# First transform of the fifth to eighth batch: three f16 products in place of one f32 product

## The chip, the cores and the metric

The kernel runs on one core of a Trainium2 chip. The metric is the device time of one execution in microseconds (us). The engines are TensorE (PE; its weight loads are listed as PEld), VectorE (DVE), ScalarE (ACT), GpSimd (POOL) and SyncE (SP, which here issues transfers).

## The reference

A two-dimensional Fourier transform is taken of each of 8 batches, its real part is kept, and the 19,968 rows go through a mixture of 8 experts, one expert for each row.

```python
X = np.fft.fft(x, axis=1)                 # x: (8, 2496, 256)
X = np.fft.fft(X, axis=2)
x = X.real.reshape(19968, 256)
logits = x @ w_gate;  e_idx = argmax(logits)
eom = sigmoid(x @ w_output_gate)
for e in range(8):
    h = np.maximum(x[mask] @ w1[e], 0.0)  # (rows, 1024)
    out[mask] = gate_w * eom[mask, e] * (h @ w2[e])
```

## The kernel before

**The transform.** Each batch is cut into five chunks of sequence positions, four of 125 and one of 128. `fold1` and `fold2` add and subtract mirrored positions (on POOL and DVE for the later batches) and leave a tile `ft` in f32. `dstage` is the first transform: TensorE multiplies `ft` (the stationary operand, 125 or 128 columns wide) by a table of cosines and sines (`tdall`, of which `tdet` and `tdab` are parts, and `tdot`), all in f32, into PSUM. For the first five batches (`b < LB`, with LB = 5) that is four f32 products of 290 columns for a chunk; for the last three it is six, of 145, 80 and 145 columns twice over. `devac` scales the result by a power of two and splits it into two f16 tiles, `ahi` (ACT) and `alo` (DVE). `sstage` is the second transform, from f16 tables and halves in three f16 products (high by high, high by low, low by high), and `sevac` turns its result into rows. `energy`, `energy_sum` and `scale` find the power of two of a batch from a sum of squares: DVE, one TensorE product, five small DVE operations. `gating` picks the expert of each row and its place, and `send` scatters the rows to DRAM (`scr`) from POOL's queue.

**The experts.** Three rounds of blocks of 512 rows for each expert, then a last phase of smaller blocks. A slot is 256 rows: `mm1` (12 products of 256 columns for a quarter of the hidden layer, f16 halves again), then ACT (`hh`) and DVE (`hl`) split its result, then `mm2`, then ACT scales it (`y`) and POOL scatters it to the output. `conv` splits a new expert's weights into f16 halves on ACT and DVE.

**What sets the order.** The transforms of the first four batches (indices 0 to 3) run ahead of the experts. From step FSTART = 14 (a step is one fifth of a batch) the transform is a background stream: each expert slot draws steps of it by fixed costs (`C_STEP`, and `C_END` = 0.05 for any other mark that the stream yields). A round of experts may load its rows once the scatters of its batches are issued. The orders on SP and POOL follow the program; those on PE, DVE and ACT are set by a scheduler as the program is built, with `behind(...)` tying an instruction behind the newest one of the experts on that engine.

Of the kernel before, what the change touches and what calls it, by code (L numbers as in the profile page):

```python
# [10 lines left out]
F16 = mybir.dt.float16  # L11
# [9 lines left out]
KC = 5  # L21
# [49 lines left out]
AHEAD = (5, 6, 7, 8, 9)  # L71

FLAG = 2

LB = BA + 3
PH1 = {mybir.EngineType.SP, mybir.EngineType.Pool}
# [169 lines left out]
def fft_moe_kernel(ctx: ExitStack, tc: tile.TileContext, xl, wg, w1, w2, tde, tdo, gt, ts0, tsm, tsr, tsq, cst, tid, out):  # L246
# [47 lines left out]
    if True:  # L294
# [114 lines left out]
        def behind(eng):  # L409
            return tc.issue_after(newest[eng]) if eng in newest else nullcontext()  # L410
# [45 lines left out]
        def fold2(b, c):  # L456
            if c == 0:
                en = en0 if b == 0 else pg.tile([128, KC], F32, name="en", tag="en")
                st[b] = {"f": {}, "en": en}
            f = st[b]["f"]  # L460
            W = slice(0, KW[c])
            ft = f[c] = pf.tile([128, 2, 2, 128], F32, name="ft", tag="ft", bufs=7)
            h = int(b >= LB)
            v = xts[b, c].rearrange("p (h a b) n -> p h a b n", h=2, a=2)[:, h]
            with behind("DVE"):
                pin(nc.vector.tensor_sub(ft[:, :, 1, W], v[:, :, 0, W], v[:, :, 1, W]))
            yield
            e = v[:, :, 0]
            with behind("DVE"):
                pin(nc.vector.tensor_add(e[:, :, W], e[:, :, W], v[:, :, 1, W]))  # L470
            if c in (0, 2):
                return
            yield
            if c == 4:
                ev, fv = (a.rearrange("p k (o h n) -> p k h o n", o=2, h=2) for a in (e, ft[:, :, 0]))
                e0, e1, fp, fm, done = ev[:, :, 0], ev[:, :, 1], fv[:, :, 0], fv[:, :, 1], (c,)
            else:
                e0 = xts[b, c - 1].rearrange("p (h a b) n -> p h a b n", h=2, a=2)[:, h, :, 0, W]
                e1, fp, fm, done = e[:, :, W], f[c - 1][:, :, 0, W], ft[:, :, 0, W], (c - 1, c)
            pin(nc.vector.tensor_add(fp, e0, e1))  # L480
            yield
            pin(nc.vector.tensor_sub(fm, e0, e1))
            for k in done:
                xts.pop((b, k))
                held[xq[b * KC + k]] -= 1
                if not hold:
                    load_x()
                if b == 0:
                    continue
                sq = pf.tile([128, 4, 128], mybir.dt.bfloat16, name="sq", tag="sq", bufs=1)  # L490
                nc.scalar.activation(sq[:, :, 0:KW[k]], f[k].rearrange("p a b n -> p (a b) n")[:, :, 0:KW[k]], AF.Square,
                                     scale=1.0 if h else 1.5, accum_out=st[b]["en"][:, k:k + 1])
# [5 lines left out]

        def energy_sum(b):
            ps = st[b]["eps"] = small()[:, 1:2]  # L500
            nc.tensor.matmul(ps, c_["ones"], st[b]["es"], start=True, stop=True)

        def scale(b):
            ps = st[b]["eps"]
            sc, iv = pow2_scale(pg, ps, 1, 11.0, "x", bufs=4, up=SH)
            lsc = pg.tile([128, 2], F32, name="lsc", tag="lsc", bufs=4)
            nc.vector.tensor_mul(lsc[:, 0:1], iv, gate["inv"])
            nc.vector.tensor_scalar(lsc[:, 1:2], lsc[:, 0:1], -1.0, None, op0=ALU.mult)
            st[b].update(sc=sc, iv=iv, lsc=lsc)
            ahi = pr.tile([128, KC, 2, 290], F16, name="ahi", tag="ahi")  # L510
            alo = pr.tile([128, KC, 2, 290], F16, name="alo", tag="alo")
            st[b].update(ahi=ahi, alo=alo)

        def dstage(b, c):
            s = st[b]
            ft = s["f"].pop(c)
            ps = pool["b"].tile([128, 2, 512], F32, name="psb_t", tag="b")
            W = slice(0, KW[c])
            for par in range(2):
                o = ps[W, par]  # L520
                if b < LB:
                    for k in range(2):
                        nc.tensor.matmul(o[:, 0:290], ft[:, k, par, W], tdab[:, k], start=(k == 0), stop=(k == 1))  # L523
                    continue
                nc.tensor.matmul(o[:, 0:145], ft[:, 0, par, W], tdet, start=True, stop=False)
                nc.tensor.matmul(o[:, 65:145], ft[:, 1, par, W], tdot[:, 0:80], start=False, stop=True)
                nc.tensor.matmul(o[:, 145:290], ft[:, 1, par, W], tdot[:, 80:225], start=True, stop=True)
            s["dps", c] = ps

        def devac(b, c):  # L530
            s = st[b]
            ps = s.pop(("dps", c))
            W = slice(0, KW[c])
            sc = s["sc"][W]
            nc.scalar.activation(s["ahi"][W, c], ps[W, :, 0:290], AF.Copy, scale=sc)  # L535
            nc.vector.scalar_tensor_tensor(s["alo"][W, c], ps[W, :, 0:290], sc, s["ahi"][W, c], op0=ALU.mult, op1=ALU.subtract)  # L536

# [558 lines left out]
        def steps():  # L1096
# [39 lines left out]
            for n in range(5 * BA, 5 * NB):  # L1136
# [16 lines left out]
                for c in ds_ if b + 1 < NB else ():  # L1153
                    dstage(b + 1, c)
                    devac(b + 1, c)
                    yield "d"
                yield from sstage(b, i)
                fillers = [piece("C")] if i or b > BA else []
                folds(n, min(KC * (b + 1) + AHEAD[i], KC + 3 * n + 2, KC * (BA + 1) + (1, 4, 4, 4, 4, 9, 99)[min(n - 5 * BA, 6)]), fillers)
# [5 lines left out]
                    pass  # L1165
                if i == 1 + (b == BA) and b + 1 < NB:
                    energy(b + 1)
                    energy_sum(b + 1)
                    scale(b + 1)
                weave(piece("A"))  # L1170
                yield ("step", n)
            add_gen(gating(NB - 1))
# [8 lines left out]
    if True:  # L1181
# [131 lines left out]
        def mm1(n, g):  # L1313
            a = sl_[n]
            T = slice(0, a["N"])
            if g % 2 == 0:
                halves(a, g // 2)
            w1v = wbuf[a["wb"]][0][g // 2].rearrange("p a (k f) -> p a k f", k=2)
            ps = psf["h"].tile([128, 2, 256], F32, name="hp", tag="h", bufs=psf["hb"])
            for k in range(2):  # L1320
                f = 2 * g + k
                m = 0
                for kc in range(2):
                    for hl, x in ((0, kc), (0, 2 + kc), (1, kc)):
                        nc.tensor.matmul(ps[:, k, T], w1v[:, hl, kc, (f % 4) * 128:(f % 4 + 1) * 128], a["x"][:, x, T], start=(m == 0), stop=(m == 5))  # L1325
                        m += 1
            G = slice(2 * (g % 2), 2 * (g % 2) + 2)
            hh, hl = a["hh", g // 2], a["hl", g // 2]
            i = nc.scalar.activation(hh[:, G, T], ps[:, :, T], AF.Relu)  # L1329
            j = nc.vector.scalar_tensor_tensor(hl[:, G, T], ps[:, :, T], 0.0, hh[:, G, T], op0=ALU.max, op1=ALU.subtract)  # L1330
            if sched[n][0] < LAST and not final:
                newest.update(ACT=getattr(i, "ins", i), DVE=getattr(j, "ins", j))

        def mm2(n, g):
            a = sl_[n]
# [252 lines left out]
```

## Time and profile before

| | us |
|---|---|
| Median of 3 runs | 1077.16 (1074.88 to 1079.08) |
| Profiled execution | 1077.15 |
| Its span | 1075.3 |
| PE busy | 1031.2 (96%) |
| DVE busy | 668.1 (62%) |
| ACT busy | 597.5 (56%) |
| POOL busy | 422.8 (39%) |

The span runs from the first to the last instruction that the profile shows, and 1.85 us of the execution lie around it. Busy is the time in which an engine has at least one instruction under way. The matmuls overlap, so what one of them costs is not its own duration but the distance from its start to the start of the next.

### The profile page before, as it was taken

Reading aid. Unit: us, or ns where it says so; the run is one execution under the profiler, and the core shown is the slowest. Engines: PE = TensorE matmul, PEld = TensorE weight load, DVE = VectorE, ACT = ScalarE, POOL = GpSimd, SP = SyncE. Lnnn points to the kernel's source line nnn. Section 1 sums busy time; section 2 is a strip of 40 time slices with the busy share of each in tenths; the row PEclk is TensorE's granted clock in tenths of the full one; section 3 lists DMA queues with packets and bytes.
Section 4 is the critical chain, followed back from the end, with each engine's and each line's share of the span. In section 5 each row is a group of like instructions: output and inputs, shape, how many; then the busy total and the mean of one; then the engine's idle time right before and its main releaser. Section 6 shows DMA issues by size and latency. Waiting matters only on the chain. (4 is left out here: it accounts for less than half of the span.)

```text
span 1075.3 us, 27862 instructions
## 1 busy us (share of the span) xinstructions
PE 1031.2 (96%) x10179; PEld 911.9 (85%) x10179; DVE 668.1 (62%) x1381; ACT 597.5 (56%) x1099; POOL 422.8 (39%) x384
## 2 busy tenths in 40 slices
PE   8888889999999999999999999999999999999997
PEld 6676768889889889988888888888999889988996
DVE  5989787786876585566586444544535455445542
ACT  3476756776775465656544555444545555445652
POOL 0068355755574572353357752221122121212121
PEclk8998989999999999999999999999999999999999
DMA  9642565675686265566556885635737766475830
GB/s 365 204 175 83 199 167 166 194 197 138 157 206 157 76 163 141 139 168 167 145 132 172 211 206 149 158 104 139 194 74 202 167 168 131 124 202 129 194 74 24
DMA packets 152312, 170.96 MB, mean 159 GB/s; under 512 B 115309, under 2 KB 116207, under 8 KB 152164
## 3 DMA queue, kind: packets, MB, share of 16 engines
q1 hardware_dynamic: 136292, 126.48, 47.2%
q0 software_dynamic: 15728, 42.14, 11.6%
q8 instruction: 82, 1.34, 0.6%
q10 hardware_dynamic: 144, 0.46, 0.2%
q14 instruction: 66, 0.54, 0.2%
HBM read 149.45 MB, written 43.63 MB: 180 GB/s over the span
## 5 line engine op out<-in xcount | busy, mean ns | idle before, releaser
L1325 PE MATMUL hp<-xr,w0b 128*128 128x256 f16 (+2 forms) x4080 | 477.4, 267 | 8.7 <-DVE hl L1330 6.9
L1347 PE MATMUL yp<-w1b,hh 128*128 128x256 f16 x2560 | 437.9, 273 | 0.0
L1325 PEld LDWEIGHTS <-w0b 128*128 128x128 f16 x4080 | 378.6, 98 | 59.8 <-issue 13.7
L1356 POOL DMA_INDIRECT out_dram<-y,xf x160 | 181.2, 1133 | 438.9 <-ACT y L1355 390.1
L1347 PE MATMUL yp<-w1b,hl 128*128 128x256 f16 x1280 | 348.9, 273 | 0.0
L1330 DVE SCALAR_TENSOR_TENSOR hl<-hp,hh 128x512 f16<-128x512 f32 (+2 forms) x340 | 221.3, 653 | 186.1 <-ACT hh L1329 162.2
L1329 ACT ACTIVATE hh<-hp 128x512 f16<-128x512 f32 (+2 forms) x340 | 192.0, 567 | 232.1 <-PE hp L1325 229.5
L1347 PEld LDWEIGHTS <-hh 128*128 128x128 f16 x2560 | 247.3, 98 | 29.9 <-issue 0.8
L749 POOL DMA_INDIRECT scr<-rows,desti x160 | 178.5, 1115 | 186.3 <-ACT rows L746 79.1
L1347 PEld LDWEIGHTS <-hl 128*128 128x128 f16 x1280 | 125.3, 98 | 14.4
L1302 DVE SCALAR_TENSOR_TENSOR w0b<-raw0b,wsc,w0b 128x1024 f16<-128x1024 f32 x44 | 60.2, 1369 | 61.5 <-ACT w0b L1300 60.4
L1355 ACT ACTIVATE y<-yp,ysc 128x256 f32<-128x256 f32 (+1 forms) x160 | 67.6, 470 | 44.0 <-PE yp L1347 34.0
L1302 DVE SCALAR_TENSOR_TENSOR w1b<-raw1b,wsc,w1b 128x1024 f16<-128x1024 f32 x44 | 57.7, 1312 | 49.5 <-ACT w1b L1300 47.1
L1300 ACT ACTIVATE w0b<-raw0b,wsc 128x1024 f16<-128x1024 f32 x44 | 50.3, 1145 | 38.8 <-PE hp L1325 37.6
L523 PE MATMUL psb_t<-tdet,ft 128*125 128x290 f32 (+1 forms) x200 | 56.2, 433 | 10.3 <-DVE ft L480 4.4
L1300 ACT ACTIVATE w1b<-raw1b,wsc 128x1024 f16<-128x1024 f32 x44 | 50.4, 1147 | 18.7 <-PE yp L1347 12.3
L523 PEld LDWEIGHTS psb_t<-tdet,ft 128*125 128x125 f32 (+1 forms) x200 | 38.7, 200 | 25.9 <-issue 8.0
L1302 DVE SCALAR_TENSOR_TENSOR w1b<-raw1b,ssc,w1b 128x1024 f16<-128x1024 f32 x32 | 41.0, 1282 | 24.6 <-ACT w1b L1300 21.1
L1302 DVE SCALAR_TENSOR_TENSOR w0b<-raw0b,ssc,w0b 128x1024 f16<-128x1024 f32 x32 | 40.8, 1282 | 21.9 <-ACT w0b L1300 21.2
L1300 ACT ACTIVATE w0b<-raw0b,ssc 128x1024 f16<-128x1024 f32 x32 | 36.3, 1144 | 14.5 <-DMA raw0b<-in_w_dram 13.4
L1300 ACT ACTIVATE w1b<-raw1b,ssc 128x1024 f16<-128x1024 f32 x32 | 36.6, 1145 | 9.9 <-DMA raw1b<-in_w_dram 6.7
L536 DVE SCALAR_TENSOR_TENSOR alo<-psb_t,p_x,ahi 125x580 f16<-125x580 f32 (+1 forms) x40 | 32.1, 817 | 15.3 <-ACT ahi L535 15.3
(232 smaller groups left out, 954.7 us busy)
## 6 DMA issues: line engine op xcount, KB each, us to landing
raw0b<-in_w_dram SPq DMA_DIRECT2D x118, 512.0 KB
raw1b<-in_w_dram SPq DMA_DIRECT2D x118, 512.0 KB
xt<-in_xl_dram SPq DMA_DIRECT2D x40, 512.0 KB
scr<-rows,desti POOLq DMA_INDIRECT x160, 3.9
out_dram<-y,xf POOLq DMA_INDIRECT x160, 3.5
xr<-scr SPq DMA_TRANSPOSE x85
xf<-scr SPq DMA_DIRECT2D x75, 2.0 KB
tst<-in_ts_dram SPq DMA_DIRECT2D x2, 512.0 KB
```

Source lines behind the costliest of these rows:

```text
L523: nc.tensor.matmul(o[:, 0:290], ft[:, k, par, W], tdab[:, k], start=(k == 0), stop=(k == 1))
L536: nc.vector.scalar_tensor_tensor(s["alo"][W, c], ps[W, :, 0:290], sc, s["ahi"][W, c], op0=ALU.mult, op1=ALU.subtract)
L749: free_order("scr", batch=b, inst=nc.gpsimd.indirect_dma_start(out=scr[:, :], out_offset=bass.IndirectOffsetOnAxis(ap=s["desti"][:, j:j + ...
L1300: nc.scalar.activation(w[:, 0], r, AF.Copy, scale=sc)
L1302: nc.vector.scalar_tensor_tensor(w[:, 1], r, sc, w[:, 0], op0=ALU.mult, op1=ALU.subtract)
L1325: nc.tensor.matmul(ps[:, k, T], w1v[:, hl, kc, (f % 4) * 128:(f % 4 + 1) * 128], a["x"][:, x, T], start=(m == 0), stop=(m == 5))
L1329: i = nc.scalar.activation(hh[:, G, T], ps[:, :, T], AF.Relu)
L1330: j = nc.vector.scalar_tensor_tensor(hl[:, G, T], ps[:, :, T], 0.0, hh[:, G, T], op0=ALU.max, op1=ALU.subtract)
L1347: nc.tensor.matmul(a["yp"][0:M, u], a[k, h][:, f, u * 128:u * 128 + M], w2v[:, hl, f], start=(g == 0 and f == 0 and m == 0), stop=(h == 1 ...
L1355: nc.scalar.activation(a["y"][0:M, u], a["yp"][0:M, u], AF.Copy, scale=ys[0:M, u:u + 1])
L1356: put = nc.gpsimd.indirect_dma_start(out=out[:, :], out_offset=bass.IndirectOffsetOnAxis(ap=a["f"].bitcast(I32)[0:M, u, 1:2], axis=0), in_ ...
```

## The change

From the fifth batch on (index 4, `HB`), `split` first scales a chunk of `ft` and splits it into two f16 tiles, `xh` on ACT and `xl` on DVE; `dhalves` then does the first transform as three f16 products for each f32 one: `xh` by the table's high half, `xh` by its low half, `xl` by its high half. `devac` no longer scales for these batches. `table_halves` splits the two tables into f16 halves and writes them over the f32 tables, in the step after the last first transform of the fourth batch; it takes two `ft` tiles as scratch. `ft` has 6 buffers in place of 7. `energy_sum` and `scale` are now tied behind the newest instruction of the experts, on PE (new) and DVE. The stream yields a mark `"x"` at every split and after every `energy`.

```diff
+HB = BA + 2
-            ft = f[c] = pf.tile([128, 2, 2, 128], F32, name="ft", tag="ft", bufs=7)
+            ft = f[c] = pf.tile([128, 2, 2, 128], F32, name="ft", tag="ft", bufs=6)
...
-            nc.tensor.matmul(ps, c_["ones"], st[b]["es"], start=True, stop=True)
+            with behind("PE"):
+                nc.tensor.matmul(ps, c_["ones"], st[b]["es"], start=True, stop=True)
...
-            sc, iv = pow2_scale(pg, ps, 1, 11.0, "x", bufs=4, up=SH)
+            with behind("DVE"):
+                sc, iv = pow2_scale(pg, ps, 1, 11.0, "x", bufs=4, up=SH)
...
+        def table_halves():
+            hi, lo = [pf.tile([128, 2, 2, 128], F32, name="ft", tag="ft", bufs=6).rearrange("p a b n -> p (a b n)").bitcast(F16)[:, 0:950] for _ in range(2)]
+            for a, o in ((tdall, 0), (tdot, 725)):
+                C = slice(o, o + a.shape[1])
+                with behind("ACT"):
+                    nc.scalar.copy(hi[:, C], a)
+                with behind("DVE"):
+                    nc.vector.tensor_sub(lo[:, C], a, hi[:, C])
+                yield
+                v = a.bitcast(F16).rearrange("p (h w) -> p h w", h=2)
+                tdh.append(v)
+                with behind("ACT"):
+                    nc.scalar.copy(v[:, 0], hi[:, C])
+                with behind("DVE"):
+                    nc.vector.tensor_copy(v[:, 1], lo[:, C])
+                yield
...
+        def split(b, c):
...
+            xh, xl_ = [pf.tile([128, 4, 128], F16, name=k, tag=k, bufs=2) for k in ("xh", "xl")]
+            with behind("ACT"):
+                nc.scalar.activation(xh[:, :, W], ft, AF.Copy, scale=s["sc"])
+            with behind("DVE"):
+                nc.vector.scalar_tensor_tensor(xl_[:, :, W], ft, s["sc"], xh[:, :, W], op0=ALU.mult, op1=ALU.subtract)
...
+        def dhalves(b, c):
...
+            terms = ((xh, 0), (xh, 1), (xl_, 0))
+            for par in range(2):
+                o = ps[0:KW[c], par]
+                if b < LB:
+                    for k in range(2):
+                        for m, (x, hl) in enumerate(terms):
+                            nc.tensor.matmul(o[:, 0:290], x[:, k, par], tdh[0][:, hl, 145 + 290 * k:435 + 290 * k], start=(k == 0 and m == 0), stop=(k == 1 and m == 2))
+                    continue
+                for m, (x, hl) in enumerate(terms):
+                    nc.tensor.matmul(o[:, 0:145], x[:, 0, par], tdh[0][:, hl, 0:145], start=(m == 0), stop=False, skip_group_check=True)
...
-            sc = s["sc"][W]
+            sc = s["sc"][W] if b < HB else 1.0
...
+                    if b + 1 >= HB:
+                        split(b + 1, c + 2)
+                        yield "x"
+                if n == 5 * HB - 6:
+                    for _ in table_halves():
+                        yield "x"
...
                     energy(b + 1)
+                    yield "x"
                     energy_sum(b + 1)
                     scale(b + 1)
+                    for c in range(2 if b + 1 >= HB else 0):
+                        yield "x"
+                        split(b + 1, c)
```

Three places show how the instructions move. On PE, at the first chunk of the sixth batch (index 5), behind a product of the experts, before:

```order
L1325 LDWEIGHTS w0b_140
L1325 MATMUL hp<-xr,w0b_140 128x256
L526 MATMUL psb_t<-tdot,ft 125x80
L527 MATMUL psb_t<-tdot,ft 125x145
L525 MATMUL psb_t<-tdet,ft 125x145
```

and now, in the same chunk (`xh` and `xl` are the f16 halves of `ft`; a LDWEIGHTS row loads the stationary operand of the MATMUL under it):

```order
L563 LDWEIGHTS xh
L563 MATMUL psb_t<-tdet,xh 125x145
L563 LDWEIGHTS xl
L563 MATMUL psb_t<-tdet,xl 125x145
L565 LDWEIGHTS xh
L565 MATMUL psb_t<-tdot,xh 125x80
```

A pair with `xh` comes twice in a row each time, then one with `xl`, for L563, L565 and L567 in turn: three products of f32 have become nine of f16, each with a load of its own of 125 columns.

On DVE, ahead of the experts, where the fourth batch is folded (L466 to L482; `rt` and `rows` belong to the second transform of the third), before:

```order
L466 TENSOR_TENSOR ft<-xt 128x2x128
L470 TENSOR_TENSOR xt<-xt 128x2x125 x2
L636 TENSOR_TENSOR rows<-rt,rows 128x4x129
L470 TENSOR_TENSOR xt<-xt 128x2x128
L480 TENSOR_TENSOR ft<-xt 128x2x125
L621 SCALAR_TENSOR_TENSOR rt<-psb_t,qb 128x2x129 x2
L480 TENSOR_TENSOR ft<-xt 128x2x2x32
L482 TENSOR_TENSOR ft<-xt 128x2x125
```

and now:

```order
L468 TENSOR_TENSOR ft<-xt 128x2x128
L525 TENSOR_TENSOR ft<-tdet,ft 128x725
L472 TENSOR_TENSOR xt<-xt 128x2x125
L525 TENSOR_TENSOR ft<-tdot,ft 128x225
L472 TENSOR_TENSOR xt<-xt 128x2x125
L694 TENSOR_TENSOR rows<-rt,rows 128x4x129
L472 TENSOR_TENSOR xt<-xt 128x2x128
L532 COPY tdot<-ft 128x225
L482 TENSOR_TENSOR ft<-xt 128x2x125
L679 SCALAR_TENSOR_TENSOR rt<-psb_t,qb 128x2x129 x2
```

Three operations of `table_halves` now stand among the folds, ahead of `rt`; the fourth, the copy of 725 columns into `tdet`, stands 20 rows further on, behind the last f32 product of the fourth batch.

On ACT, among the experts, at the first chunks of the fifth batch (`ahi` is the evacuation of its first transform), before:

```order
L1355 ACTIVATE y<-yp,ysc 128x256
L535 ACTIVATE ahi<-psb_t,p_x 125x580 x2
L1355 ACTIVATE y<-yp,ysc 128x256
L1300 ACTIVATE w1b_142<-raw1b_138,wsc 128x1024
L1329 ACTIVATE hh<-hp 128x512
```

and now:

```order
L1397 ACTIVATE hh<-hp 128x512
L545 ACTIVATE xh<-ft,p_x 128x4x125 x2
L1397 ACTIVATE hh<-hp 128x512
L1346 ACTIVATE wsq,wen<-raw0b_136 128x1024
L545 ACTIVATE xh<-ft,p_x 128x4x125
L593 ACTIVATE ahi<-psb_t 125x580
L545 ACTIVATE xh<-ft,p_x 128x4x125
L593 ACTIVATE ahi<-psb_t 125x580
```

Four splits now stand among the evacuations of the first two chunks and the experts' `hh`; the splits run two chunks ahead of the products.

## Rows read from the trace of the kernel before

**Rows 1.** Busy time of each engine in two stretches (with instruction counts, granted clock).

```profile
core 0: us, PE busy (x) PEld busy (x) DVE busy (x) ACT busy (x) POOL busy (x), PEclk, DMA share, GB/s
100.00:165.00 65.00, 54.95 (x442) 44.23 (x443) 53.44 (x133) 42.95 (x92) 30.27 (x23) 0.90 0.60 173
165.00:460.00 295.00, 290.50 (x2883) 258.23 (x2881) 210.61 (x452) 189.98 (x371) 165.01 (x150) 1.00 0.60 155
```

**Rows 2.** Waits of PE from 165 to 460 us (total us, times, longest).

```profile
PE hp L1325 <- DVE hl L1330: 3.2, 5, 1.1
PE psm_t L394 <- DVE web L393: 0.6, 1, 0.6
PE hp L1325 <- ACT y L1355: 0.6, 1, 0.6
```

**Rows 3.** Timeline of PE, fifth batch (start, duration, what, how many records).

```profile
176.22 3.10 PE L523 MATMUL psb_t<-tdet,ft 128*125 128x290 f32 x12
179.16 1.47 PE L1325 MATMUL hp<-xr,w0b 128*128 128x256 f16 x12
180.47 1.14 PE L523 MATMUL psb_t<-tdet,ft 128*125 128x290 f32 x4
```

**Rows 4.** Timeline of PE, sixth batch: one half of a chunk, and the next's start.

```profile
235.06 0.41 PE L525 MATMUL psb_t<-tdet,ft 128*125 128x145 f32 x2
...
235.77 0.41 PE L525 MATMUL psb_t<-tdet,ft 128*125 128x145 f32 x2
```

**Rows 5.** Timeline of PE: two runs of f16 products, 16 and 145 columns wide.

```profile
59.88 0.20 PE L568 MATMUL psm_t<-ahi,tstq 125*128 125x16 f16 x2
...
60.72 0.17 PE L568 MATMUL psm_t<-ahi,tstq 128*128 128x16 f16 x1
...
167.73 0.23 PE L591 MATMUL psb_t<-ahi,tstr 125*128 125x145 f16 x1
...
169.65 0.38 PE L1347 MATMUL yp<-w1b,hh 128*128 128x256 f16 x2
```

**Rows 6.** Timeline of weight loads (PEld).

```profile
234.49 0.30 PEld L526 LDWEIGHTS psb_t<-tdot,ft 128*125 128x125 f32 x2
234.71 0.30 PEld L527 LDWEIGHTS psb_t<-tdot,ft 128*125 128x125 f32 x2
...
1065.50 0.14 PEld L1347 LDWEIGHTS <-hh 128*64 128x64 f16 x2
```

**Rows 7.** Groups by shape, of weight loads (count; busy us, mean ns).

```profile
L526 PEld LDWEIGHTS psb_t<-tdot,ft 128*125 128x125 f32 x48 | 7.4, 188 | 0.0
L1347 PEld LDWEIGHTS <-hh 128*64 128x64 f16 x16 | 1.7, 110 | 0.1
```

**Rows 8.** Timeline of PE and DVE ahead of the experts ([idle before, releaser]).

```profile
101.53 6.49 PE L523 MATMUL psb_t<-tdet,ft 128*125 128x290 f32 x16 [4.37 <-DVE ft L480]
102.97 1.86 DVE L448 TENSOR_TENSOR xt<-xt 128x500 f32<-128x500 f32 x3
...
105.43 1.08 DVE L466 TENSOR_TENSOR ft<-xt 128x250 f32<-128x250 f32 x3
...
109.25 2.20 PE L523 MATMUL psb_t<-tdet,ft 128*125 128x290 f32 x8 [1.22 <-DVE rt L621]
```

**Rows 9.** Groups by shape: a cast on ACT, a subtraction on DVE.

```profile
L636 DVE TENSOR_TENSOR rows<-rt,rows 128x516 f16<-128x516 f32 x40 | 29.0, 725 | 7.1 <-ACT rows L635 7.1
L635 ACT CAST rows<-rt 128x516 f16<-128x516 f32 x40 | 25.0, 625 | 17.4 <-DVE rt L633 15.5 <-DVE rt L621 1.7
```

**Rows 10.** Timeline of POOL and SP: last scatter for the second round, its first rows.

```profile
319.08 0.98 POOL L749 DMA_INDIRECT scr<-rows,desti  x1 [0.30 <-issue]
...
326.97 1.26 SPq L1255 DMA_TRANSPOSE xr<-scr  x1
```

**Rows 11.** Scales of the last phase by line: duration min/median/max, first and last start.

```profile
L812 DVE TENSOR_REDUCE ssc<-r_p x3: 477/486/488, 570.2 to 573.4; 128x40 f32<-128x320 f32 x3
```

**Rows 12.** The last phase's loads of weights by line, in the same columns.

```profile
L1272 SPq DMA_DIRECT2D raw0b<-in_w_dram x74: 73/84/363, 700.5 to 1039.3; - x74
```

More of the change, by code (lines that the diff above doesn't have):

```diff
@@ new lines, in fft_moe_kernel @@
+        tdh = []
+        def split(b, c):
+            if c >= KC:
+                return
+            s = st[b]
+            W = slice(0, KW[c])
+            ft = s["f"].pop(c).rearrange("p a b n -> p (a b) n")[:, :, W]
+            xh, xl_ = [pf.tile([128, 4, 128], F16, name=k, tag=k, bufs=2) for k in ("xh", "xl")]
[3 more added lines that the diff above has]
+                nc.vector.scalar_tensor_tensor(xl_[:, :, W], ft, s["sc"], xh[:, :, W], op0=ALU.mult, op1=ALU.subtract)
+            s["xs", c] = [a.rearrange("p (k r) n -> p k r n", k=2)[:, :, :, W] for a in (xh, xl_)]
@@ new lines, in dhalves @@
+        def dhalves(b, c):
+            s = st[b]
+            xh, xl_ = s.pop(("xs", c))
+            ps = pool["b"].tile([128, 2, 512], F32, name="psb_t", tag="b")
+            terms = ((xh, 0), (xh, 1), (xl_, 0))
[8 more added lines that the diff above has]
+                    nc.tensor.matmul(o[:, 0:145], x[:, 0, par], tdh[0][:, hl, 0:145], start=(m == 0), stop=False, skip_group_check=True)
+                for m, (x, hl) in enumerate(terms):
+                    nc.tensor.matmul(o[:, 65:145], x[:, 1, par], tdh[1][:, hl, 0:80], start=False, stop=(m == 2), skip_group_check=True)
+                for m, (x, hl) in enumerate(terms):
+                    nc.tensor.matmul(o[:, 145:290], x[:, 1, par], tdh[1][:, hl, 80:225], start=(m == 0), stop=(m == 2))
+            s["dps", c] = ps
@@ L514, in dstage @@
         def dstage(b, c):
+            if b >= HB:
+                return dhalves(b, c)
             s = st[b]
@@ L1324, in mm1 @@
                     for hl, x in ((0, kc), (0, 2 + kc), (1, kc)):
-                        nc.tensor.matmul(ps[:, k, T], w1v[:, hl, kc, (f % 4) * 128:(f % 4 + 1) * 128], a["x"][:, x, T], start=(m == 0), stop=(m == 5))
+                        l = nc.tensor.matmul(ps[:, k, T], w1v[:, hl, kc, (f % 4) * 128:(f % 4 + 1) * 128], a["x"][:, x, T], start=(m == 0), stop=(m == 5))
                         m += 1
@@ L1331, in mm1 @@
             if sched[n][0] < LAST and not final:
-                newest.update(ACT=getattr(i, "ins", i), DVE=getattr(j, "ins", j))
+                newest.update(PE=getattr(l, "ins", l), ACT=getattr(i, "ins", i), DVE=getattr(j, "ins", j))
         def mm2(n, g):
```

## The prediction

> **What bounds the kernel now.** I read the table by stretches first. From 165 to 460 us, where the transforms of the last batches run among the experts, PE is busy for 290.5 of 295 us at the full clock of 2.4 GHz (granted 1.00), DVE for 71% and ACT for 64% [rows 1]; what PE waits for there adds up to 4.4 us, nearly all of it for DVE [rows 2]. So in this stretch a microsecond of products taken away is a microsecond of the end, and work added on DVE or ACT costs only what it makes PE wait. From 100 to 165 us it is otherwise: PE stands still for 10 us and the clock is at 0.90 in the mean [rows 1]. There the reader should see two gaps of PE that end with DVE [rows 8]; what is added to DVE between them is paid in full. After 460 us only experts and the end of the transform are left, and nothing is changed.
>
> The profiled execution took 1077.15 us, the median of the runs is 1077.16, so I sum against 1077.15. A difference of less than 0.5% (5.4 us) can't be told from none.
>
> **The products.** The distance from start to start is the price. In the fifth batch 12 records, which are 6 products of f32 (two records each), fill 179.16 - 176.22 = 2.94 us, so 0.49 us for 290 columns; the 12 products of f16 with 256 columns behind them take 180.47 - 179.16 = 1.31, so 0.109 each [rows 3]. Thirty f16 products of 145 columns take 1.92 us, 0.064 each, and 33 of 16 columns 0.84, 0.025 each [rows 5]. From 145 to 256 columns a column costs 0.0004 us, so a product of 290 takes 0.123. For the fifth batch 5 chunks x 2 halves x 2 = 20 f32 products (9.8 us) become 60 of f16 (7.4 us): 2.4 us less.
>
> For the last three batches one half of a chunk (145, 80 and 145 columns) takes 235.77 - 235.06 = 0.71 us [rows 4], and there are 3 x 5 x 2 = 30 halves. Now each has six f16 products of 145 columns and three of 80. By the slope a product of 80 columns costs 0.038. But no f16 product of before has a stationary operand of 125 columns, and the loads decide how close short products may follow each other. Here the rows go apart:
> - f32 loads of 125 columns: two, of 0.188 each [rows 7], fill 0.30, and the next pair starts 0.22 after the first pair [rows 6]. They follow each other at 0.11 us.
> - f16 loads that are not 128 wide: the one case has 64 columns. Two, of 0.110 each [rows 7], fill 0.14 [rows 6], so the second starts 0.03 after the first. By columns, 125 would need 0.03 x 125 / 64 = 0.059.
> I take 0.059, since the type is the same and the f32 row differs in type as well as in width: 0.064 for 145 columns stays, 80 columns cost 0.059. A half is 6 x 0.064 + 3 x 0.059 = 0.56 for the 24 halves of 125 columns; for the 6 halves of 128 columns, whose loads look like those of the experts, 6 x 0.064 + 3 x 0.038 = 0.50. Saved: 24 x 0.15 + 6 x 0.21 = 4.9 us. Together 7.3 us. The bounds: all loads hidden, 30 x 0.21 + 2.4 = 8.8 saved; loads at the f32 pace, 9 x 0.11 = 0.98 for a half, 24 x 0.27 = 6.5 lost against 2.4 + 1.3 gained, so 2.8 us more than before.
>
> What the row shows for a load of 64 columns is 0.03 us. The Trainium skill, "TensorE: Matmul & The Clock Gate", section "LDWEIGHTS (loading the stationary operand)", gives columns / 1.2 in ns, which is 104 ns for 125 columns, and its section on weight-path modes keeps the fast load for f16 weights of exactly 128. By that, an estimate, nearly all of the new products would be held to 104 ns and the sum would be a loss of some 2 us; the row of 64 columns speaks against it (53 ns by that rule), the f32 row for it. It is the third rival.
>
> **The tables.** `table_halves` is eight operations once. Three of those on DVE stand among the folds of the fourth batch, between PE's gaps of 4.37 and 1.22 us, and the second gap ends with `rt`, which is behind them [rows 8]. Three additions of 500 columns take 1.86 us, three of 250 columns 1.08 [rows 8], so a column costs 0.001 us: 0.85 for 725, 0.33 for 225, and 0.2 for the f16 copy of 225 (between nothing and 0.33). That is 1.4 us on a chain on which PE waits. The casts on ACT (0.625 for 516 columns [rows 9], so about 0.8 and 0.3) stand where ACT waits for DVE. The copies into `tdet` must wait for the last f32 product of the fourth batch, as the evacuation behind them does, and hold it up by up to 0.8; the experts begin then and cover most of that, so I take 0.3. In all 1.7 us; bounds 0 (another wait covers it) and 2.2. PE's second gap grows from 1.2 to 2.6 us; after the gap of 4.37 us eight products took 6.49, 0.81 each [rows 8], at the lower clock. Were the clock to fall here too, the four products behind it would cost 1.3 more.
>
> **The splits.** Twenty on ACT, 20 on DVE. The nearest rows are a cast of 516 columns, 0.625 us, and an f32 subtraction to f16, 0.725 [rows 9]: 12.5 and 14.5 us, which take ACT from 64% to 69% and DVE from 71% to 76% [rows 1]. The cover is the experts' products. The products of a chunk now wait for `xh` and `xl`, and behind them on PE, which takes its instructions in order, stand the experts. The new marks thin the stream: 32 marks of 0.05 against 25 steps of some 0.9, so 7% more slots for the same batches, and DVE's share comes back to 72%. If PE's 4.5 us of waiting grows as DVE's free share shrinks (29% to 28%), little is added; with 20 new places at which PE can be too early I take 0.5. Bounds: nothing, and 5.8 if in each of the four batches two splits of five fall where DVE has no free time and both engines' costs of a split pass through (4 x 2 x 0.725).
>
> **At nothing.** One buffer of `ft` fewer: a chunk's `ft` is now free after its split, and never more than six are live. `devac` without its scale is the same instruction. The scatters of the fourth batch come later by one group of four, some 5 us, behind more output scatters on POOL's queue; the first load of rows for the second round is 6.9 us behind the last of them now [rows 10] and would wait on SP, with the weight loads behind it, if the margin went; two slots lie between that load and its use, and they hide it. The transform ends later by some slots, but the scales of the last phase are there at 573.4 us and its first weights are loaded at 700.5 [rows 11, 12].
>
> **Sum.** 1077.15 - 7.3 + 1.7 + 0.5 = 1072.0 us.
>
> **Rivals.**
> 1. *All loads hidden and the tables covered*: 8.8 saved, 0.4 paid, 1068.8 us. For it: the 16-column row shows that f16 loads of 128 columns cost no more than 0.025. Against it: none of those is 125 wide.
> 2. *The splits contend*: 5.8 us of waiting instead of 0.5, 1077.3 us; no change. For it: what PE waits for is DVE already. Against it: 84 us of DVE's stretch are free.
> 3. *The loads bound the new products* (slower): nine loads of 0.11 in each of the 24 narrow halves, 2.8 us lost, with tables and splits 1077.15 + 2.8 + 1.7 + 0.5 = 1082.2. The fifth batch and the six halves of 128 gain 2.4 + 1.3 = 3.7, of which tables and splits leave 1.5; a pace of 0.086 us a load takes that away, 24 x (9 x 0.086 - 0.71) = 1.5, and from there on the kernel is slower than before. For it the f32 loads, against it the 64-column ones.
> 4. *Rows or weights of a round come late, or the clock falls*: 1084 and more. Nothing in the rows asks for it.
>
> **How the numbers follow.** The forecast 0.50, with its own range 1069.5 to 1075; rival 1 0.20, rival 2 0.15, rival 3 0.10, rival 4 0.05. Faster by over 0.5% means below 1071.8: nearly half of the forecast and rival 1, 0.44. Within 0.5%: the rest of the forecast, rival 2 and part of rival 3, which lies on the bound, 0.45. Slower 0.11. The range that leaves out no more than 2 in 10 runs from 1067 to 1080.
>
> **What would show it.** In the changed kernel's timeline a half of a chunk of the sixth to eighth batch should take 0.56 us where nothing interrupts it, and 0.37 for three products of 290 columns; weight loads of 125 columns should follow each other at 0.06. If they stand 0.11 apart, rival 3 holds. The table operations should lengthen PE's gap before the last f32 products ahead of the experts by about 1.4 us. PE's waits in the stretch of the splits should be near 5 us; if `xh` or `xl` lead the list of what PE waits for, rival 2 holds. The prediction is wrong if PE's busy time falls by 7 us and the end does not follow.

## The result, and the profile after

The changed kernel takes 1083.75 us in the median of 10 runs (1078.92 to 1087.24), the kernel before in the same comparison 1076.91 (1074.78 to 1079.08): ratio 1.0058, interval 1.0046 to 1.0071 (a ratio here is taken over the runs; the quotient of the two medians is 1.0063). It is slower by 6.8 us, where 5.1 us faster was forecast. The profiled execution took 1081.47 us with a span of 1079.6, so the two profiled executions lie 4.3 us apart.

By stretches, in the columns of [rows 1]; the second row covers all of the time in which transforms and experts run together, of this kernel and then of the kernel before:

```profile
165.00:465.00 300.00, 289.27 (x3004) 258.44 (x3004) 226.57 (x473) 200.95 (x390) 156.53 (x145) 1.00 0.59 157
118.00:600.00 482.00, 464.20 (x4710) 410.61 (x4707) 352.50 (x797) 304.42 (x589) 241.32 (x222) 0.99 0.60 160
```

```profile
118.00:600.00 482.00, 472.60 (x4630) 417.72 (x4629) 341.71 (x777) 296.27 (x573) 255.13 (x230) 0.99 0.62 163
```

PE stands still for 482 - 464.2 = 17.8 us from 118 to 600 us, before for 9.4. DVE and ACT gained 11 and 8 us of work there and are at 73% and 63%, far from full. The granted clock is 0.99 in both. What ended PE's waits from 165 to 465 us (total us, times, longest), beside [rows 2]:

```profile
PE yp L1415 <- ACT y L1423: 3.4, 5, 1.7
PE hp L1393 <- DVE hl L1398: 3.4, 6, 1.2
PE yp L1415 <- DVE w1b L1370: 1.5, 1, 1.5
PE hp L1393 <- ACT w0b L1368: 1.3, 1, 1.3
PE yp L1415 <- ACT w1b L1368: 0.9, 1, 0.9
```

One entry more, of 0.8 us, is PE's wait for itself. Neither `xh` nor `xl` is in the list. PE waits nearly 11 us for the experts' own evacuations and weights, which come late; before it was 4.4.

The products themselves, in PE's timeline: the first three records of a half of 125 positions, the same of the next half, and what follows them; then the same of a chunk of 128; then one run of three products of 290 columns and the start of the next:

```profile
460.86 0.29 PE L563 MATMUL psb_t<-tdet,xh 128*125 128x145 f16 x2
...
461.41 0.29 PE L563 MATMUL psb_t<-tdet,xh 128*125 128x145 f16 x2
...
461.97 1.25 PE L1393 MATMUL hp<-xr,w0b 128*128 128x256 f16 x10
...
480.03 0.29 PE L563 MATMUL psb_t<-tdet,xh 128*128 128x145 f16 x2
...
480.52 0.29 PE L563 MATMUL psb_t<-tdet,xh 128*128 128x145 f16 x2
...
203.93 0.41 PE L560 MATMUL psb_t<-tdet,xh 128*128 128x290 f16 x2
...
204.30 0.41 PE L560 MATMUL psb_t<-tdet,xh 128*128 128x290 f16 x2
```

A half costs 0.555 us (0.56 was forecast), a half of 128 positions 0.49 (0.50), three products of 290 columns 0.37 (0.37). Taken for all halves of their kind, the fifth batch's 60 products take 7.4 us for 9.8, and the last three batches gain 24 x 0.155 + 6 x 0.22 = 5.0: 7.4 us of products are saved, as forecast. The loss is elsewhere.

The tables, in the timelines of DVE (three operations) and PE (the two runs of f32 products ahead of the experts), beside [rows 8]:

```profile
106.92 0.91 DVE L525 TENSOR_TENSOR ft<-tdet,ft 128x725 f16<-128x725 f32 x1
...
108.07 0.38 DVE L525 TENSOR_TENSOR ft<-tdot,ft 128x225 f16<-128x225 f32 x1
...
109.65 0.21 DVE L532 COPY tdot<-ft 128x225 f16<-128x225 f16 x1
```

```profile
102.03 7.14 PE L581 MATMUL psb_t<-tdet,ft 128*125 128x290 f32 x16 [4.37 <-DVE ft L482]
111.00 2.20 PE L581 MATMUL psb_t<-tdet,ft 128*125 128x290 f32 x8 [1.83 <-DVE rt L679]
```

DVE's chain grew by 1.5 us (1.4 was forecast). From the start of the first gap to the second run of products it is 13.34 us, before 12.09, so 1.25 us are paid at this place. The eight products between the gaps took 0.65 us more, but not for the tables: in b_marks (below), which has no table operation, they took 7.15 us and the second gap was 0.57, so beside it the whole 1.25 lies in the gap. That the 1.25 us reach the end isn't shown: the first product of the experts starts at 124.14 us here, at 122.27 in the kernel before and at 124.36 in b_marks.

### The profile page after: what moved, and what is told of

The parts are those of the page before. It is cut to its first block, busy times and chain, and to the rows that moved or that the text cites. A ratio compares the mean times of both kernels' runs of the same rounds, so it can differ in the third digit from the quotient of the medians.

```text
span 1079.6 us, 28120 instructions
## 1 busy us (share of the span) xinstructions
PE 1029.8 (95%) x10289; PEld 909.8 (84%) x10289; DVE 682.0 (63%) x1405; ACT 609.8 (56%) x1123; POOL 418.5 (39%) x384
## 5 line engine op out<-in xcount | busy, mean ns | idle before, releaser
L1424 POOL DMA_INDIRECT out_dram<-y,xf x160 | 178.2, 1114 | 426.5 <-ACT y L1423 378.6
L1398 DVE SCALAR_TENSOR_TENSOR hl<-hp,hh 128x512 f16<-128x512 f32 (+2 forms) x340 | 221.1, 653 | 183.3 <-ACT hh L1397 159.3
L1370 DVE SCALAR_TENSOR_TENSOR w0b<-raw0b,wsc,w0b 128x1024 f16<-128x1024 f32 x44 | 56.9, 1293 | 60.1 <-ACT w0b L1368 57.9
L581 PE MATMUL psb_t<-tdet,ft 128*125 128x290 f32 (+1 forms) x160 | 50.2, 476 | 10.8 <-DVE rt L679 4.4
L581 PEld LDWEIGHTS psb_t<-tdet,ft 128*125 128x125 f32 (+1 forms) x160 | 34.5, 222 | 24.9 <-issue 7.6
L693 ACT CAST rows<-rt 128x516 f16<-128x516 f32 x40 | 25.0, 626 | 18.0 <-DVE rt L691 15.0
```

Source lines behind the costliest of these rows:

```text
L693: nc.scalar.copy(rows[:, :, :, 0:129], t)
L1370: nc.vector.scalar_tensor_tensor(w[:, 1], r, sc, w[:, 0], op0=ALU.mult, op1=ALU.subtract)
L1424: put = nc.gpsimd.indirect_dma_start(out=out[:, :], out_offset=bass.IndirectOffsetOnAxis(ap=a["f"].bitcast(I32)[0:M, u, 1:2], axis=0), in_ ...
```

## The experiments

Ratios are to the kernel before on the same chip. The kernels marked * ran on chips on which the kernel before itself takes 1122 to 1135 us, so their times can't be set beside 1077; only their ratios are used.

| kernel | median us | ratio (interval) |
| --- | --- | --- |
| b_marks | 1077.57 | 0.9995 (0.9986 to 1.0005) |
| b_ties | 1077.79 | 1.0003 (0.9992 to 1.0014) |
| a_marks0 | 1083.67 | 1.0047 (1.0033 to 1.0062) |
| a_noxl | 1082.43 | 1.0039 (1.0024 to 1.0053) |
| after_2 | 1082.38 | 1.0054 (1.0036 to 1.0072) |
| a_wait32_2 | 1087.93 | 1.0099 (1.0082 to 1.0116) |
| a_nowait_2 | 1081.13 | 1.0031 (1.0017 to 1.0045) |
| a_early0 | 1084.98 | 1.0059 (1.0037 to 1.0081) |
| a_wait32* | 1152.38 | 1.0176 (1.0136 to 1.0217) |
| a_nowait* | 1142.73 | 1.0089 (1.0060 to 1.0119) |
| a_hb5* | 1134.56 | 1.0025 (0.9993 to 1.0056) |
| b_tab* | 1135.44 | 1.0020 (0.9989 to 1.0051) |
| b_wait* | 1134.10 | 1.0111 (1.0083 to 1.0139) |
| b_act* | 1129.32 | 1.0063 (1.0033 to 1.0093) |
| b_ft6* | 1121.42 | 1.0003 (0.9979 to 1.0026) |
| a_hb5_2* | 1125.95 | 1.0046 (1.0023 to 1.0068) |
| b_wait_2* | 1145.09 | 1.0073 (1.0036 to 1.0109) |
| b_act_2* | 1136.53 | 1.0037 (1.0005 to 1.0069) |

**The schedule, the ties, DVE's half of the split.** Two theories stood against each other: the added marks and ties move work about, or the splits load DVE and ACT.

b_marks:

```diff
                     devac(b + 1, c)
                     yield "d"
+                    if b + 1 >= BA + 2:
+                        yield "x"
+                if n == 5 * (BA + 2) - 6:
+                    for _ in range(4):
+                        yield "x"
...
                     energy(b + 1)
+                    yield "x"
                     energy_sum(b + 1)
                     scale(b + 1)
+                    for c in range(2 if b + 1 >= BA + 2 else 0):
+                        yield "x"
```

> The kernel before, with only the new marks "x" in the stream of steps: nothing is split, no product or table is changed, the energies are not tied. If the changed kernel lost its gain because the marks spread the transform over more slots and so moved its pieces among the experts, this takes 1081 to 1085 us. If the splits' work on DVE and ACT is the cause, or the ties, it stays at 1077 within 2 us.

b_ties:

```diff
-            nc.tensor.matmul(ps, c_["ones"], st[b]["es"], start=True, stop=True)
+            with behind("PE"):
+                nc.tensor.matmul(ps, c_["ones"], st[b]["es"], start=True, stop=True)
...
-            sc, iv = pow2_scale(pg, ps, 1, 11.0, "x", bufs=4, up=SH)
+            with behind("DVE"):
+                sc, iv = pow2_scale(pg, ps, 1, 11.0, "x", bufs=4, up=SH)
```

> The kernel before, with only the ties: the product of the energies behind the newest expert product on PE, the power-of-two scale behind the newest expert evacuation on DVE. If the ties are the cause (each of four batches waits a microsecond or two at them), 1081 to 1084 us; if the marks or the splits are, 1077 within 2 us.

a_marks0:

```diff
-C_STEP, C_TAB, C_END, C_SCAT = {"d": 0.1, "s": 0.27, "step": 0.26}, 0.03, 0.05, 0.8
+C_STEP, C_TAB, C_END, C_SCAT = {"d": 0.1, "s": 0.27, "step": 0.26, "x": 0.0}, 0.03, 0.05, 0.8
```

> The changed kernel with marks that cost nothing, so that the splits come in the same slot as the piece before them and the transform takes as many slots as before the change. If the spreading by the marks is the cause, the 7 us of the products come through: 1074 to 1077 us. If the splits' work is the cause, it is now packed closer and waits more: 1084 us or more.

a_noxl:

```diff
-            terms = ((xh, 0), (xh, 1), (xl_, 0))
+            terms = ((xh, 0), (xh, 1), (xh, 1))
...
-            with behind("DVE"):
-                nc.vector.scalar_tensor_tensor(xl_[:, :, W], ft, s["sc"], xh[:, :, W], op0=ALU.mult, op1=ALU.subtract)
```

> The changed kernel without the low half of the split: the operation on DVE is left out, and the third product uses the high half and the table's low half a second time (the same number of products and loads). If the splits' work on DVE is the cause, 14.5 us of DVE are taken out and the time falls to 1076 to 1078 us; if marks or ties are, it stays at 1082 to 1085.

Neither marks nor ties alone cost anything that can be measured, and marks that cost nothing bring nothing back. Without the 20 operations on DVE, some 16 us of its time from 118 to 600 us, the median is 1.3 us lower than the changed kernel's in the result and level with that of after_2; by the ratios it is better by 1.5 to 2 us, and the intervals overlap. Both theories as I had them fall: most of the loss is in neither.

**The wait for the scale.** Before, a chunk's products need only `ft`; now they need the batch's energies, their scale and a split by it. a_wait32 keeps the new wait and the f32 products, a_nowait keeps the f16 products and drops the wait for the scale; a_hb5 starts one batch later; b_tab prices the tables.

a_wait32 and a_wait32_2:

```diff
-            xh, xl_ = [pf.tile([128, 4, 128], F16, name=k, tag=k, bufs=2) for k in ("xh", "xl")]
+            xs = pf.tile([128, 4, 128], F32, name="xh", tag="xh", bufs=2)
             with behind("ACT"):
-                nc.scalar.activation(xh[:, :, W], ft, AF.Copy, scale=s["sc"])
-            with behind("DVE"):
-                nc.vector.scalar_tensor_tensor(xl_[:, :, W], ft, s["sc"], xh[:, :, W], op0=ALU.mult, op1=ALU.subtract)
+                nc.scalar.activation(xs[:, :, W], ft, AF.Copy, scale=s["sc"])
...
-            if b >= HB:
-                return dhalves(b, c)
             s = st[b]
-            ft = s["f"].pop(c)
+            ft = s.pop(("xs", c)) if b >= HB else s["f"].pop(c)
```

> The changed kernel's waits with the products of before: from the fifth batch on ACT copies a chunk with its scale into an f32 tile, and the f32 products of before read that tile; no low halves, no split tables (their four marks stay). If the loss comes from the products' new wait for the batch's scale and a copy (in the order of PE the fifth batch's first product stands behind 277 expert products instead of 170), the new stalls of PE come with the products' full price: 1082 to 1087 us. If it comes from f16 products, splits on DVE or tables, this stays at 1077 to 1079.

> The kernel a_wait32 once more, on a chip on which the kernel before takes its usual 1077 us: f32 products that wait for the scale and a copy, no low halves, no split tables. If the products' wait and later place are the cause: 1082 to 1087 us, no less than the changed kernel. If f16 products, splits on DVE or tables are: 1077 to 1079.

a_nowait and a_nowait_2:

```diff
-                nc.scalar.activation(xh[:, :, W], ft, AF.Copy, scale=s["sc"])
+                nc.scalar.copy(xh[:, :, W], ft)
...
-                nc.vector.scalar_tensor_tensor(xl_[:, :, W], ft, s["sc"], xh[:, :, W], op0=ALU.mult, op1=ALU.subtract)
+                nc.vector.tensor_sub(xl_[:, :, W], ft, xh[:, :, W])
...
-            sc = s["sc"][W] if b < HB else 1.0
+            sc = s["sc"][W]
```

> The changed kernel with halves split without the batch's scale, which goes into the evacuation again as before: the products need only ft and its two halves, not the energies (the fifth batch's first product stands behind 211 expert products). Values of this input are split unscaled. If the wait for the scale is the cause, the gain comes through in part: 1074 to 1078 us. If the amount of work on DVE and ACT or the tables are, 1082 to 1085.

> The kernel a_nowait once more on such a chip: halves split without the batch's scale, so that the products don't wait for the energies. If that wait is the cause: 1074 to 1078 us; if the amount of work on DVE and ACT or the tables are: 1082 to 1085.

a_early0 has in addition the splits of chunks 0 and 1 ahead of `energy(b + 1)` and `"x": 0.0`.

> As a_nowait, with the first two splits of a batch written ahead of its energies, and with marks that cost nothing: the f16 products stand nearly where the f32 products of before stand (the fifth batch's first behind 211 expert products instead of 170, the sixth's 720 instead of 708, the seventh's 1296 instead of 1200, the eighth's 1968 instead of 1916). If the place of the products is the cause, this is the fastest of the four, 1072 to 1076 us. If the splits and tables themselves cost what the products save, it stays at 1081 or more.

after_2 is the changed kernel, beside them:

> The changed kernel once more, so that the three kernels beside it are compared on one chip: 1.0046 to 1.0071 of before, as in the result.

a_hb5 and a_hb5_2:

```diff
-HB = BA + 2
+HB = BA + 3
```

> The changed kernel from the sixth batch on instead of the fifth: 5.1 us of products gained instead of 7.5, the tables split in the experts' time. If the fifth batch's stretch (142 to 170 us, where DVE is behind) makes most of the loss, this takes 1075 to 1078 us. If each batch loses alike, 1080 to 1083.

> The kernel a_hb5 once more on a chip at its usual time: halves from the sixth batch on, the fifth stays in f32 and doesn't wait. If the wait is the cause, the fifth batch's gaps (3.5 to 4.5 us near 160) are gone, but 2.4 us of gain too: 1077 to 1080. If the loss has nothing to do with the wait, 1082 or more.

b_tab has `table_halves` added to the kernel before at its place, with the second four operations into a third `ft` tile:

> The kernel before, with the tables' eight operations added at their place and their result unused (the second four write into a spare tile instead of the tables, so that they do not wait for the last f32 product). By the prediction's term 1.2 to 1.7 us more than before, 1078.2 to 1078.7; if the gap of PE that they lengthen also lowers the clock, 1080 or more.

a_wait32_2 is the decisive one: with no f16 product, no low half and no split table, it is 11.0 us slower than before. PE's standstill from 118 to 600 us is 482 - 464.6 = 17.4, the same as in the changed kernel; in b_marks it is 9.1, as before. The windows of a_wait32_2, then of b_marks:

```profile
118.00:600.00 482.00, 464.58 (x4530) 408.97 (x4531) 336.25 (x771) 301.94 (x584) 237.08 (x218) 0.99 0.60 156
```

```profile
118.00:600.00 482.00, 472.92 (x4618) 417.75 (x4615) 338.74 (x778) 294.77 (x571) 243.97 (x223) 0.99 0.62 160
```

DVE has no more work there than in b_marks, ACT 7 us more. Gap by gap, a_wait32_2 has seven of over 0.5 us that b_marks lacks (0.94, 1.49, 0.89, 1.50, 1.31, 1.70 and 0.84, together 8.7 us), b_marks has one of 1.28 that a_wait32_2 lacks, and their profiled executions lie 8.8 us apart. Beside b_marks it has the wait, the copies on ACT, the ties and the smaller `ft`; the last two alone cost nothing (b_ties, b_ft6). So the standstill comes from the wait, or from the copies on ACT, or from both.

a_nowait_2 gives 1.3 us (medians) to 2.5 us (ratios, 1.0054 to 1.0031) back, less than expected, and the two intervals overlap. Its trace shows where it falls short. Its products stand over the squares of the fifth batch again (157.08 to 162.39 us), and the changed kernel's gaps of 0.63, 1.49 and 1.69 us, shown below, are gone; but the two at `w1b` are 1.19 and 2.22 us for 0.89 and 1.48, and behind the second the granted clock is 0.51 from 168.8 to 172.0 us, so PE runs nearly all of it at 1.2 GHz, where the changed kernel has 1.00. PE's standstill from 118 to 600 us is 15.4 us for 17.8. a_early0 should have been the fastest and isn't: its products stand nearly where those of before stand, but now PE reaches them ahead of their halves. PE's timeline of a_early0 ([idle before, releaser]):

```profile
241.15 0.34 PE L563 MATMUL psb_t<-tdet,xh 128*125 128x145 f16 x2 [1.63 <-ACT xh L545]
...
328.50 0.34 PE L563 MATMUL psb_t<-tdet,xh 128*125 128x145 f16 x2 [0.91 <-ACT xh L545]
...
330.30 0.28 PE L563 MATMUL psb_t<-tdet,xl 128*125 128x145 f16 x1 [1.46 <-DVE p_x L291]
```

Early products wait for their split, late ones leave PE without them when it needs them. The clock falls behind its longer gaps, too: it is granted at 0.86 and 0.80 from 160 to 170 and from 170 to 180 us, and at 0.83 from 240 to 250 and from 330 to 340, where the changed kernel has 1.00. Counted as (1 - clock) x 10 us, an estimate, that is 6.8 us from 120 to 600 us, against 3.4 in the changed kernel (0.66 from 140 to 150). So the place alone is not the cure that I expected. a_hb5_2 (slower by 0.2 to 0.7%) and b_tab (no more than 0.5%) leave their questions where they were: with the fifth batch in f32 there is still no gain.

**The wait, the copies and the buffer apart.** Each is added to the kernel before; b_wait and b_act have ties and marks too.

b_wait (its `split` stands where the changed kernel has it):

```diff
+        def split(b, c):
...
+            ft = s["f"][c][:, 0, 0, 0:1]
+            if c == 0:
+                s["iw"] = pg.tile([128, 1], F32, name="iw", tag="iw", bufs=2)
+                nc.vector.tensor_scalar(s["iw"], s["iv"], 2.0 ** -SH, None, op0=ALU.mult)
+            with behind("DVE"):
+                nc.vector.scalar_tensor_tensor(ft, ft, s["sc"], s["iw"], op0=ALU.mult, op1=ALU.mult)
```

> The kernel before with ties and marks, and the wait for the scale alone: f32 products from ft, but an operation on DVE writes one column of each chunk of ft with the batch's scale and its inverse (the value stays), in the place of the split, so that the products can't start ahead of the scale. No copy on ACT, seven buffers of ft. The fifth batch's first product stands behind 252 expert products instead of 170, the sixth's 853 instead of 708. If the wait and the later place are the cause: 1083 to 1088 us, with PE's new gaps near 160 and 230 to 255 us. If the copies on ACT or the buffer are: 1077 to 1079.

> The kernel b_wait once more, on a chip at its usual time if there is one. If the wait and the later place of the products make the loss: 1083 to 1088 us, with gaps of PE near 160 and 230 to 255 us. If the copies do: 1077 to 1079.

b_act:

```diff
+        def split(b, c):
...
+            xh = pf.tile([128, 4, 128], F16, name="xh", tag="xh", bufs=2)
+            with behind("ACT"):
+                nc.scalar.activation(xh[:, :, W], ft, AF.Copy, scale=s["sc"])
```

> The kernel before with ties and marks, and the 20 copies on ACT alone, into a tile that nothing reads: 12.5 us more on ACT, the products wait for nothing new. If ACT's load is the cause: 1083 to 1088 us. If the wait is: 1077 to 1079.

> The kernel b_act once more, on a chip at its usual time if there is one. If the copies on ACT make the loss: 1083 to 1088 us. If the wait does: 1077 to 1079. If both count, this takes 1079 to 1082 and b_wait_2 some 1082.

b_ft6:

```diff
-            ft = f[c] = pf.tile([128, 2, 2, 128], F32, name="ft", tag="ft", bufs=7)
+            ft = f[c] = pf.tile([128, 2, 2, 128], F32, name="ft", tag="ft", bufs=6)
```

> The kernel before with six buffers of ft instead of seven; the order on the engines stays. If the folds wait for a buffer and DVE's queue with them: 1080 us or more. If the prediction was right that none is missed: 1077 within 1 us.

Both kernels were slower than before, the wait by 1.1 and 0.7%, the copies by 0.6 and 0.4%; the buffer costs nothing that can be measured. In the traces the wait can be told from the copies. The larger gaps of PE in the changed kernel, in a_wait32_2, in b_wait and in b_act (timeline, 140 to 290 us):

```profile
162.66 1.49 PE L1393 MATMUL hp<-xr,w0b 128*128 128x256 f16 x12 [1.49 <-DVE hl L1398]
165.03 0.27 PE L1415 MATMUL yp<-w1b,hh 128*128 128x256 f16 x1 [0.89 <-ACT w1b L1368]
166.78 0.27 PE L1415 MATMUL yp<-w1b,hh 128*128 128x256 f16 x1 [1.48 <-DVE w1b L1370]
...
253.12 0.38 PE L1415 MATMUL yp<-w1b,hh 128*128 128x256 f16 x2 [1.69 <-ACT y L1423]
```

```profile
160.00 1.48 PE L1389 MATMUL hp<-xr,w0b 128*128 128x256 f16 x12 [0.94 <-DVE hl L1394]
162.97 1.48 PE L1389 MATMUL hp<-xr,w0b 128*128 128x256 f16 x12 [1.49 <-DVE lsc L511]
...
242.30 0.39 PE L1389 MATMUL hp<-xr,w0b 128*128 128x256 f16 x2 [1.31 <-ACT w0b L1364]
...
255.78 0.38 PE L1411 MATMUL yp<-w1b,hh 128*128 128x256 f16 x2 [1.70 <-ACT y L1419]
```

```profile
177.04 1.49 PE L1348 MATMUL hp<-xr,w0b 128*128 128x256 f16 x12 [0.94 <-DVE hl L1353]
180.02 1.48 PE L1348 MATMUL hp<-xr,w0b 128*128 128x256 f16 x12 [1.49 <-DVE hl L1353]
...
258.44 0.39 PE L1348 MATMUL hp<-xr,w0b 128*128 128x256 f16 x2 [1.28 <-ACT w0b L1323]
...
271.93 0.38 PE L1370 MATMUL yp<-w1b,hh 128*128 128x256 f16 x2 [1.69 <-ACT y L1378]
```

```profile
171.90 0.16 PE L394 MATMUL psm_t<-web,cs 128*128 128x1 bf16 x1 [0.74 <-DVE web L393]
...
212.14 0.38 PE L1347 MATMUL hp<-xr,w0b 128*128 128x256 f16 x2 [0.84 <-issue]
```

Gaps of 0.94, 1.49, 1.28 to 1.31 and 1.69 us stand in a_wait32_2 and in b_wait, which shares with it the wait, the marks and the ties but no copy on ACT; b_act, with marks, ties and copies, has none of them. So they don't need the copies. Not all of them are the wait's alone, though. b_ties, which has no wait and loses nothing, has one like that of 1.49, in the fifth batch too:

```profile
164.38 1.47 PE L1327 MATMUL hp<-xr,w0b 128*128 128x256 f16 x12 [1.51 <-DVE lsc L510]
```

And the gap of 1.31 us at `w0b` stands in a_nowait_2 as well (at 240.22 us). Those of 0.94 near 160 us and of 1.69 at `y` are in none of the profiled kernels whose products don't wait for the scale.

The two gaps of 0.89 and 1.48 us at `w1b` (0.89 and 1.50 in a_wait32_2) are not in b_wait, and its timelines of PE and DVE show why. DVE's work on `w1b` is as late there, but eight f32 products, which wait for the scale and for no copy, stand over it:

```profile
181.34 4.08 PE L536 MATMUL psb_t<-tdet,ft 128*125 128x290 f32 x16
...
182.38 3.38 DVE L1325 SCALAR_TENSOR_TENSOR w1b<-raw1b,wsc,w1b 128x1024 f16<-128x1024 f32 x2
```

In a_wait32_2 DVE's work on `w1b` starts at 165.33 us, and the fifth batch's first product, which waits for a copy that starts only at 166.71, comes at 169.73, behind both gaps. So these two belong to the products' wait for their copy or split. Where the copies in b_act cost their 0.4 to 0.6% isn't shown, and on a chip at 1077 us only the sum of wait and copies was measured (a_wait32_2, 1.0%).

## Why the prediction was wrong

**Products: right.** 7.3 us forecast, 7.4 measured. (By its own terms the prediction's upper bound of 8.8 is 8.7 and its 9 x 0.11 is 0.99; the forecast rests on neither.) The third rival, that the loads bound the products at the f32 pace of 0.11, falls: nine products of a half fill 0.555 us. In the loads' groups by shape (busy us, mean ns) one f16 load of 125 columns is a record of 137 ns, more than the 104 ns that the rule named beside that rival gives (the Trainium skill, "TensorE: Matmul & The Clock Gate", "LDWEIGHTS (loading the stationary operand)"), but the loads overlap, and with nine products in 0.555 us they follow each other at 0.062 in the mean:

```profile
L563 PEld LDWEIGHTS <-xh 128*125 128x125 f16 x48 | 5.4, 137 | 0.1
```

**Tables: right, a little high.** 1.25 us at the gap for which 1.4 was forecast; the 0.3 for the copies into `tdet` wasn't measured by itself.

**At nothing: right for the buffer** (b_ft6), and each by itself for the ties, which the prediction doesn't name, and the marks (b_ties, b_marks). The later scatters and scales cost nothing to be seen: from 465 to 800 us PE is never still in either trace.

**Splits: wrong, and here the sign was lost.** The step was: "The cover is the experts' products", with 0.5 us for "20 new places at which PE can be too early" and a bound of 5.8. It was about 13: the change of the medians is 6.8, and 6.8 + 7.4 - 1.25 = 12.9. a_wait32_2 measures 11.0 for the wait and the copies together, with f32 products; what DVE's half adds is not clear of the noise (a_noxl, nothing to 2 us). The operations themselves were 13.9 us on ACT and 17.1 on DVE for 12.5 and 14.5, and DVE's share from 165 to 465 us is 76%, not back at 72%; but that is not what PE waits for. Of the loss the traces place less than the medians ask for: between the two profiled executions the same sum is 4.3 + 7.4 - 1.25 = 10.5, and PE's standstill grew by 8.4.

I had counted the wait as if only the waiting product could come too late. The products waited for are also a cover: in the kernel before they keep PE busy while ACT and DVE do the energies and folds of that batch. The timelines of PE and ACT of the kernel before show it:

```profile
155.46 3.10 PE L523 MATMUL psb_t<-tdet,ft 128*125 128x290 f32 x12
...
156.10 0.62 ACT L491 ACTIVATE sq<-ft 128x500 bf16<-128x500 f32 x1
...
156.72 0.57 ACT L1329 ACTIVATE hh<-hp 128x512 f16<-128x512 f32 x1
157.20 0.61 ACT L491 ACTIVATE sq<-ft 128x500 bf16<-128x500 f32 x1
...
157.93 0.63 ACT L491 ACTIVATE sq<-ft 128x512 bf16<-128x512 f32 x1
```

Six f32 products of the fifth batch run from 155.46 to 158.40, over the three squares of its energies. In the changed kernel these products can't start before the sum of the squares is scaled (PE, ACT, and one line of DVE):

```profile
157.57 1.48 PE L1393 MATMUL hp<-xr,w0b 128*128 128x256 f16 x12
159.68 1.49 PE L1393 MATMUL hp<-xr,w0b 128*128 128x256 f16 x12 [0.63 <-DVE hl L1398]
...
158.46 0.62 ACT L493 ACTIVATE sq<-ft 128x500 bf16<-128x500 f32 x1
...
159.20 0.62 ACT L493 ACTIVATE sq<-ft 128x500 bf16<-128x500 f32 x1
...
159.94 0.63 ACT L493 ACTIVATE sq<-ft 128x512 bf16<-128x512 f32 x1
...
161.28 0.59 ACT L1397 ACTIVATE hh<-hp 128x512 f16<-128x512 f32 x1
...
166.38 1.32 ACT L545 ACTIVATE xh<-ft,p_x 128x500 f16<-128x500 f32 x2
...
158.95 0.67 DVE L1398 SCALAR_TENSOR_TENSOR hl<-hp,hh 128x512 f16<-128x512 f32 x1
```

PE has only expert products over the squares. It waits twice. The first gap, of 0.63 us, ends with an `hl` whose `hh` was there at 156.74, but which stands on DVE behind the folds of that batch until 158.95. The second, of 1.49 us ([1.49 <-DVE hl L1398] above), ends with the `hl` of the next `hh`, and that `hh` stands on ACT behind the three squares and two `y` until 161.28. The first split starts at 166.38, after both: no split's duration, on ACT or DVE, can have made them. In the order on PE the first product of the fifth batch moved from behind 170 to behind 277 expert products. This is the mechanism at one place, and the gaps at `w1b`, which b_wait's products cover and a_wait32_2's don't, are a second. That it makes the other gaps too is argued from their equality in a_wait32_2 and b_wait, not shown one by one.

**The rivals.** The second (splits contend, 1077.3) named the right engines and the wrong reason, and with less than half the price. What it said would decide, `xh` or `xl` at the head of PE's waits, did not come, and the loss came all the same. The first falls with the tables' 1.25 us and the half of 0.555. The fourth named nearly the measured time, by luck: taken in tens of microseconds, the granted clock from 120 to 600 us is under 1.00 only from 140 to 150 (0.66), before as now, and PE's list has no wait for rows or for a transfer; its waits at `w0b` and `w1b` are for the splitting of the weights on ACT and DVE.

**What stays open.** The copies' share and its place; whether marks and ties together, which were measured only one by one, add to b_wait and b_act; where the part of the loss lies that the standstill doesn't hold; and what the products' early place would give if PE neither reached them ahead of their halves nor lost its clock. No version that was run beats the kernel before.

## What to carry to other kernels

Work on a saturated engine is not only a cost: where it needs nothing from the engines that are behind, it is what keeps the engine busy while they catch up. Before giving such work a new input, look in the timeline at what the other engines do while it runs, and price the stretch without it, not only the wait itself. A busy share of 71% over 295 us said nothing about the 10 us in which evacuations queue behind a burst.

## What the runs showed of the hardware

On the chips of the kernels marked *, PE waits often for nothing that the profile shows ("issue"); the kernel before, profiled on a chip at 1077 us, has no such line among PE's waits. PE's waits in b_ft6 (total us, times, longest):

```profile
PE psb_t L594 <- issue: 11.8, 18, 1.1
PE psb_t L602 <- issue: 8.2, 12, 1.6
PE hp L1325 <- issue: 5.8, 15, 0.6
```

These add up to 25.8 us in a kernel that takes 1121 us there, some 44 more than the kernel before at its usual time; what the chip does in them no run tells.
